# Moving the V loads of a cached-attention decode kernel from SyncE's DMA queue to ScalarE's

## The chip, the cores and the metric

The kernel runs on one core of a Trainium2 chip. The metric is device time in microseconds (us), lower is better, as the median of several executions. On one core a run counts as slow when it is over 1.5% above the fastest of the same kernel. In the profiles PE is TensorE, DVE VectorE, ACT ScalarE and SP SyncE; PEld is TensorE's weight load, and SPq and ACTq are the DMA issues of SyncE and ScalarE.

## The reference, cut to what matters

One decode step: four sequences, one new token each, attention over a window of cached keys and values, plus a gated feed-forward block on the same normalized input.

```python
B, Sq, D = 4, 1, 640
Hq, Hkv, Sk, Dh = 32, 32, 8192, 192        # window W = 2048 of 8192 positions
xn = layernorm(x)
q = (xn @ wq) per head
scores = einsum("bhqd,bhkd->bhqk", q, k[last W]) * Dh ** -0.5
o = einsum("bhqk,bhkd->bhqd", softmax(scores), v[last W])
return x + o.reshape(B, 1, Hq * Dh) @ wo + (silu(xn @ w1) * (xn @ w3)) @ w2
```

K and V are bf16. Per head, the four sequences' windows are 3.15 MB of K and 3.15 MB of V. Over 32 heads that is 201 MB, read once; with the weights 223 MB. There is little arithmetic per byte, so the DMA is the first suspect.

## The kernel before

Head by head, K and V arrive as one tile each of 128 partitions x 24,576 bytes. VectorE multiplies K by the broadcast q in four quarters; TensorE and VectorE reduce the products to scores; ScalarE takes the exponential; TensorE multiplies by V ("PV", into `o_ps`); ScalarE copies the result to `o_raw`.

```python
KBUFS = 2; VBUFS = 3; L = 10; GQ = 4      # a head is GQ = 4 slots
kpool = tile_pool(name="kt", bufs=KBUFS)
vpool = tile_pool(name="vt", bufs=VBUFS)

def load_k(h):
    kt = kpool.tile([P, NJ, Dh], BF16, tag="kt")
    nc.sync.dma_start(out=kt..., in_=k_win[:, h]...)
def load_v(h, pieces=1):
    vt = vpool.tile([P, NJ, Dh], BF16, tag="vt")
    ...
        nc.sync.dma_start(out=vt..., in_=src...)
# wo_load, ffn_load, w2_load, and the loads of x and Wq: nc.sync.dma_start too
...
for h in range(H):
    u0, ul = h * GQ, h * GQ + GQ - 1
    if h >= KBUFS:
        add((h - KBUFS + 1) * GQ, 0, load_k, h)       # K(h): after the last multiply of head h-2
    add(h * GQ + (2 if h != H - 3 else 5), 0, load_v, h, 1 if h < H - 1 else 2)
    ...                                              # multiply, add, reduce, softmax
    add(u0 + L, 3, pv, h, 0)                          # PV ten slots after the head began
    add(u0 + L + 2, 3, pv, h, 1)                      # its end frees V's buffer
for hg in range(NG):                                  # 8 groups of 4 heads
    add(hg * HG * GQ + 8 if hg < NG - 1 else NU, 0, wo_load, hg)
    ...
add(f, 0, ffn_load, "w1", B_w1)                       # f: head 6
add(f + 6, 8, ffn_load, "w3", B_w3)
add(NU + 2, 1, w2_load, [(0, FC // 2), (FC // 2, FC - 2), (FC - 2, FC)])
```

`add(slot, phase, ...)` fixes each engine's program order; semaphores fix the time. So a K issue waits for VectorE to free one of two buffers, and a V issue for a PV that frees one of three.

## Time and profile before

| | before |
|---|---|
| median of 4 runs | 533.83 us (532.94 to 534.59) |
| span of the profiled run | 533.2 us |
| VectorE busy / PE busy / ScalarE busy | 349 / 391 / 48 us |
| last byte loaded (from the packet records; the recorded texts have 524.6 and 524.7) | 525.5 us |

The page's table of DMA queues (bytes moved, and packet time as a share of 16 engines' span):

```profile
q1 hardware_dynamic: 11680, 222.97, 97.8%
```

The table of stretches of the kernel before: stretch, its length, busy time of PE, PEld, DVE, ACT and GpSimd (with their instructions), the clock granted to TensorE, DMA share, GB/s.

```profile
40.00:110.00 70.00, 50.16 (x331) 21.27 (x329) 50.65 (x64) 4.83 (x16) 0.00 (x0) 0.80 1.01 432
110.00:180.00 70.00, 51.68 (x379) 22.45 (x378) 43.06 (x58) 11.52 (x25) 0.00 (x0) 0.85 1.00 431
390.00:460.00 70.00, 50.07 (x378) 22.08 (x377) 44.62 (x61) 5.01 (x20) 0.00 (x0) 0.80 1.00 430
460.00:500.00 40.00, 32.73 (x237) 14.16 (x237) 30.71 (x40) 1.96 (x8) 0.00 (x0) 0.75 0.96 410
```

The DMA engines never rest from 40 to 460 us; the kernel is bound by bytes over rate. A line of the waits list of the kernel before (who waited for whom, us in total, times, longest):

```profile
DVE pr L202 <- DMA kt<-in_A_k_cache_dram: 99.2, 29, 7.9
```

And the last line of the view of the V tile of the same kernel:

```profile
DMA to landing us min/median/max: 12.5/25.6/30.3
```

VectorE waits for K 29 times in 32 heads. A V tile needs 25.6 us from issue to landing although its bytes take 7.3 us at 430 GB/s. The rest it stands in the queue, behind other tiles.

### The profile page before, as it was taken

The page shows a single profiled execution, that of the slowest core. Times are in us where ns is not written, and L with a number is a line of the kernel's source. Part 1 is how long each engine was busy: PE and PEld are TensorE (multiplying, and loading weights), DVE is VectorE, ACT ScalarE, POOL GpSimd, SP SyncE. Part 2 cuts the span into 40 slices and gives each one's busy share as a digit, 9 for nine tenths or more (in the row PEclk, how much of TensorE's full clock was granted, in tenths as well). Part 3 has the DMA queues.
Part 4 walks back from the last instruction along what each step waited for, and adds up shares of the span by engine and source line. Part 5 has one row for each costly group of instructions (what it writes and reads, how often), then busy time and mean ns, then how long its engine had stood idle before and what let it go on. Part 6 is the DMA issues. An engine that isn't in the chain of part 4 may idle for free.

```text
span 533.2 us, 6724 instructions
## 1 busy us (share of the span) xinstructions
PE 391.0 (73%) x2949; PEld 177.6 (33%) x2949; DVE 349.4 (66%) x471; ACT 48.2 (9%) x150; POOL 1.1 (0%) x8
## 2 busy tenths in 40 slices
PE   2876776867686978676947688586749868587987
PEld 0322232333142433232413334233313324232544
DVE  3177775787384776776757777578657778477860
ACT  2111000000222000000000000000000000000010
POOL 0000000000000000000000000000000000000000
PEclk9879776899698797688989969689996769777998
DMA  8999999999999999999999999999999999998993
GB/s 353 430 428 431 421 442 424 438 435 428 425 435 432 428 433 431 431 427 439 429 428 431 435 426 438 430 428 435 430 433 428 433 428 440 435 420 372 422 390 140
DMA packets 11709, 223.39 MB, mean 419 GB/s; under 512 B 1304, under 2 KB 1312, under 8 KB 2720
## 3 DMA queue, kind: packets, MB, share of 16 engines
q1 hardware_dynamic: 11680, 222.97, 97.8%
q8 instruction: 23, 0.38, 0.3%
q14 instruction: 6, 0.05, 0.0%
HBM read 222.96 MB, written 0.01 MB: 418 GB/s over the span
## 4 chain that ended last, share of the span: by engine, by line
DMA 59%; DVE 22%; PE 17%; issue 1%; ACT 0%; SPq 0%
DMA kt<-in_A_k_cache_dram 56%; DVE pr L202 17%; PE ps L213 7%; PE gp L294 5%; DVE sc L221 4%; DMA wt<-in_A_wq_dram 3%; PE qps L172 2%; PE o_ps L266 1%; PE acc_239 L194 1%; PE acc_240 L195 1%; DVE oT L303 1%; DVE rtb L284 1%; DVE qbc L178 0%; ACT o_raw L272 0%; DVE o_ps L186 0%
## 5 line engine op out<-in xcount | busy, mean ns | idle before, releaser
L213 PE MATMUL ps<-pr,idb 128*128 128x512 bf16 x768 | 228.9, 445 | 119.8 <-DVE sc L221 116.3
L202 DVE TENSOR_TENSOR pr<-kt,qbc 128x3072 bf16<-128x3072 bf16 x128 | 223.9, 1750 | 100.2 <-DMA kt<-in_A_k_cache_dram 99.2
L213 PEld LDWEIGHTS <-idb 128*128 128x128 bf16 x768 | 79.5, 108 | 219.8 <-issue 166.7
L221 DVE TENSOR_REDUCE sc<-ps 128x16 f32<-128x512 f32 x128 | 87.5, 684 | 10.1 <-PE ps L213 9.1
L266 PE MATMUL o_ps<-vt,z 128*8 128x384 bf16 x1024 | 59.3, 356 | 0.0
L294 PEld LDWEIGHTS gp<-sel,o_raw 128*32 128x32 f32 x768 | 46.8, 151 | 21.3 <-issue 19.2
L272 ACT COPY o_raw<-o_ps 128x384 f32<-128x384 f32 x32 | 15.3, 479 | 405.4 <-PE o_ps L266 405.4
L294 PE MATMUL gp<-sel,o_raw 128*32 128x4 f32 x768 | 49.6, 199 | 1.1 <-ACT o_raw L272 0.6
L266 PEld LDWEIGHTS <-z 128*8 128x8 bf16 x1024 | 21.1, 89 | 41.6 <-issue 32.6
L284 DVE RECIPROCAL rtb<-mt 32x4 f32<-32x4 f32 x32 | 5.7, 179 | 32.2 <-PE gp L294 31.9
L172 PE MATMUL qps<-wt,xnT 128*128 128x512 bf16 x60 | 17.7, 463 | 4.9 <-DMA wt<-in_A_wq_dram 4.9
L178 DVE CAST qbc<-qps 128x512 bf16<-128x512 f32 x6 | 3.8, 684 | 19.4 <-PE qps L172 19.4
L257 DVE TENSOR_TENSOR z<-ex,mask_b 128x256 bf16<-128x256 bf16 x32 | 13.2, 414 | 2.4 <-ACT ex L249 2.4
L194 PE MATMUL acc_239<-wo_t,oT 128*4 128x320 bf16 x48 | 13.8, 305 | 0.3 <-DVE oT L303 0.3
L195 PE MATMUL acc_240<-wo_t,oT 128*4 128x320 bf16 x48 | 13.8, 306 | 0.0
L243 PEld LDWEIGHTS mt<-ones_ff,gneg 1*128 1x128 f32 x64 | 9.4, 182 | 10.2 <-issue 9.6
L243 PE MATMUL mt<-ones_ff,gneg 1*128 1x1 f32 x64 | 12.1, 256 | 0.0
L172 PEld LDWEIGHTS <-xnT 128*128 128x128 bf16 x60 | 6.9, 115 | 15.3 <-issue 10.2
L249 ACT ACTIVATE ex<-sc,negm 128x64 bf16<-128x64 f32 x32 | 11.1, 348 | 1.0
L326 PE MATMUL gt<-w_756,xnT 128*4 128x512 bf16 x15 | 6.9, 622 | 4.2 <-DVE oT L303 2.9
L230 PE MATMUL mt<-idf,lmax 128*1 128x128 f32 x32 | 9.2, 287 | 0.0
L235 DVE TENSOR_REDUCE gmax<-mt 1x4 f32<-1x128 f32 x32 | 8.6, 269 | 0.7 <-PE mt L230 0.7
(59 smaller groups left out, 98.4 us busy)
## 6 DMA issues: line engine op xcount, KB each, us to landing
kt<-in_A_k_cache_dram SPq DMA_DIRECT2D x32, 3072.0 KB, 20.5
vt<-in_A_v_cache_dram SPq DMA_DIRECT2D x31, 3072.0 KB, 25.7
wo_t<-in_A_wo_dram SPq DMA_DIRECT2D x8, 960.0 KB, 19.4
wt<-in_A_wq_dram SPq DMA_DIRECT2D x2, 3072.0 KB, 9.8
vt<-in_A_v_cache_dram SPq DMA_DIRECT2D x2, 1536.0 KB, 14.1
w_756<-in_B_w_dram SPq DMA_DIRECT2D x1, 1920.0 KB, 23.4
w_1001<-in_B_w_dram SPq DMA_DIRECT2D x1, 1920.0 KB
wt<-in_A_wq_dram SPq DMA_DIRECT2D x1, 1536.0 KB, 19.8
```

The source lines that it names most:

```text
L172: nc.tensor.matmul(qp[:], lhsT=xnT[:, kc].rearrange("p a b -> p (a b)"), rhs=wq_rows[kc][:, (c0 + i) * QC:(c0 + i + 1) * QC], start=(kc == ...
L194: nc.tensor.matmul(acc0[:], lhsT=lhsT, rhs=rhs[:, 0:N0], start=first, stop=last)
L195: nc.tensor.matmul(acc1[:], lhsT=lhsT, rhs=rhs[:, N0:D], start=first, stop=last)
L202: nc.vector.tensor_tensor(out=pr[:], in0=kts[h][:, g * JQ:(g + 1) * JQ, :], in1=qbc[:, h * Dh:(h + 1) * Dh].unsqueeze(1).to_broadcast([P, ...
L213: nc.tensor.matmul(ps[:], lhsT=idb[:], rhs=pr[:, :, kk * DD:(kk + 1) * DD], start=(kk == 0), stop=(kk == NK - 1))
L221: nc.vector.tensor_reduce(out=scs[h][:, g * JQ:(g + 1) * JQ], in_=pss.pop(u)[:], axis=AX.X, op=ALU.add)
L243: nc.tensor.matmul(mt[:, P:P + 1], lhsT=gneg[:].rearrange("o p b -> o (p b)"), rhs=ones_ff[0:1, 0:1], start=True, stop=True)
L249: nc.scalar.activation(out=ex[:], in_=scs.pop(h)[:], func=ACTF.Exp, bias=negm[:, 0:1], scale=SCALE, accum_out=rsum[:])
L257: nc.vector.tensor_tensor(out=z[:], in0=ex[:].unsqueeze(2).to_broadcast([P, NJ, B]), in1=mask_b[:].unsqueeze(1).to_broadcast([P, NJ, B]), ...
L266: nc.tensor.matmul(o_ps[c * CT:c * CT + 2 * B, :], lhsT=z[:, 2 * jj:2 * jj + 2, :], rhs=vt[:, 2 * jj:2 * jj + 2, :], start=(jj < 4), stop= ...
L272: nc.scalar.copy(out=o_raw[:].rearrange("q two d -> q (two d)"), in_=o_ps[:])
L294: nc.tensor.matmul(gp[sl, i, :], lhsT=o_raw[:, part, i:Dh:RPP], rhs=sel[:, part * B:(part + 1) * B], start=(part == 0), stop=(part == 1))
```

## The change

The intent: V gets a queue of its own, so that V and K need not stand behind each other and SyncE's waits for K buffers do not hold up V.

```diff
-            nc.sync.dma_start(out=vt[:, i * n:(i + 1) * n, :].rearrange("q j d -> q (j d)"),
+            nc.scalar.dma_start(out=vt[:, i * n:(i + 1) * n, :].rearrange("q j d -> q (j d)"),
                               in_=src[:, :, i * n:(i + 1) * n, :].rearrange("p b j d -> p b (j d)"))
```

## The prediction

> **What bounds the kernel now.** The DMA engines. The queue table has SyncE's queue busy for 97.8% of the span, 418 GB/s in the mean; a table of stretches shows 430 to 432 GB/s from 13 to 460 us. The chain of waits is 56% "DMA kt", and the waits list has VectorE idle 99 us for K. VectorE needs 10.9 us of work per head (349 us / 32); K and V of a head (6.29 MB) need 14.6 us at 430 GB/s. Bytes stop at about 524.6 us; the last 8.6 us are a PE chain (last PV, o_raw, gp, oT, Wo and W2 products).
>
> **What the change does.** No byte and no compute instruction goes. 33 V issues (0.54 us each, 18 us) move from SyncE to ScalarE, which is 9% busy. SyncE's waits before V issues go, but cost nothing now: K lands 20.5 us and V 25.7 us after issue, so the queue is never empty. On ScalarE a V issue meets no new wait: its buffer is freed by PV matmuls whose o_raw copy ScalarE has already waited for. It comes 1.2 to 2.7 us later (o_raw 0.48, negm 0.17, exp 0.35, its accumulator 0.19, sometimes a table load 1.28).
>
> Order changes. One FIFO of K, V, K, V becomes two queues. The Trainium skill, "DMA: Bandwidth & Descriptors", section "Issuing engines are not separate DMA queues", says both run on the same 16 engines and interleave: no bandwidth gained; section "Queues, rings and completion order" has each engine alternate between queues by packet. This trace has one data queue and cannot confirm it. A K tile then flows at half rate, for 14.6 us instead of 7.3, but continuously: VectorE still gets one K per 14.6 us. The steady state stays equal.
>
> **Where I expect a loss.**
> 1. Weights sit on K's queue, so K falls behind V around W1, W3 and Wo; V fills its buffers and stops issuing. The backlog at a K issue, now about 11 us (3.6 of the K before, 7.3 of V), shrinks to an estimated 3 to 5 us, so pauses around the FFN (VectorE idle 8.6 us behind PE near 146 us) may leave bubbles: 0 to 3 us.
> 2. The end. Now the order is K31, V29, V30, V31, Wo, W2. Afterwards SyncE issues Wo and W2 right behind K31 (about 486 us instead of 504), competing with V30 and V31. K31 lands an estimated 2 us later than needed (503 against 500.7 us), V31 at an estimated 522 to 525 us, where the last PV now starts at 519.7. As 9 to 10 us of PE work follow, that adds 2 to 5 us.
>
> The start gains nothing: V0 goes out after ScalarE's qbc copies (31 us instead of 26.8), still before the queue is empty (about 34 us).
>
> **Predicted time:** 538 us, range 532 to 546. Faster by over 2%: 0.02; within 2%: 0.87; slower by over 2%: 0.11.
>
> **What would show it.** Two data queues, V's 101 MB on the second; about 430 GB/s from 13 to 460 us; V issued on ScalarE; VectorE idle behind K 100 to 110 us; Wo 7 and W2 issued near 486 us; the last PV 2 to 5 us later, after a wait for V, with V among the last bytes.
>
> **What would make it wrong.** Two interleaved streams moving at another rate than one (2% of rate is about 10 us); a share between the queues far from equal; ScalarE blocked at a V issue so that exp and o_raw come late; mid-run bubbles over 3 us.

## The result, and the profile after

The changed kernel takes 558.70 us (median of 4 runs, 554.50 to 559.21) against 533.83: a ratio of 1.0449, 95% interval 1.0396 to 1.0503. Ratios here are the mean time of one kernel's fast runs over that of the other's of the same rounds, so not quite the ratio of the medians. It is slower by 4.5%, outside the predicted range. The result stays correct.

The queue table of the kernel after:

```profile
q1 hardware_dynamic: 6928, 122.30, 52.5%
q10 hardware_dynamic: 4752, 100.67, 42.1%
```

The same bytes on two queues, and the shares now add up to 94.6% of a longer span. The table of stretches:

```profile
40.00:110.00 70.00, 46.80 (x306) 20.09 (x305) 47.26 (x61) 4.83 (x16) 0.00 (x0) 0.76 1.00 422
110.00:180.00 70.00, 47.01 (x348) 20.12 (x346) 38.71 (x51) 11.53 (x25) 0.00 (x0) 0.88 0.95 399
390.00:460.00 70.00, 48.52 (x388) 22.37 (x386) 44.68 (x61) 5.10 (x20) 0.00 (x0) 0.83 0.97 411
460.00:500.00 40.00, 24.89 (x225) 12.26 (x225) 27.59 (x37) 1.96 (x8) 0.00 (x0) 0.91 0.97 407
500.00:510.00 10.00, 8.10 (x68) 4.21 (x68) 9.55 (x14) 0.98 (x4) 0.00 (x0) 1.00 0.65 242
```

Every stretch moves less than before. A finer view tells a lower rate from pauses: the same window of 80 us in 40 slices of 2 us, before and after (first row busy tenths of the DMA engines, second row GB/s).

```profile
DMA  9999999999999999999999999999999999999999
GB/s 406 418 442 467 430 406 414 442 467 418 406 418 455 467 418 406 418 467 415 403 480 426 422 406 418 504 418 414 393 430 504 406 418 406 430 504 406 418 406 438
```

```profile
DMA  9999999999999268999999999999999999999999
GB/s 462 467 426 406 393 455 479 430 406 393 455 479 430 123 172 356 451 406 467 406 430 442 418 467 406 430 438 406 416 405 508 441 393 442 418 467 438 393 446 406
```

These are 400 to 480 us. Outside a hole of 5 us at 426 us (123, 172, 356 GB/s) the two move at the same pace. So the streams do not disturb each other; the engines now and then have nothing to do. Summing over all packet records how far the rate of each half microsecond fell short of its median, where it was under 80% of it (median 432 GB/s in both kernels; the first 5 us left out):

```
         lost in gaps   where (us from the start: us lost)
before      2.7 us      483-487: 1.9   510-513: 0.7
after      19.1 us      103-109: 1.2   148-155: 5.1   240-244: 1.3   303-305: 0.7   364-367: 0.7
                        426-431: 2.6   490-494: 1.7   499-506: 4.9   and two of 0.3 to 0.4 at the end
```

The last byte loaded comes at 543.0 us instead of 525.5 (17.5 us later, of which the gaps are 16.4), and the work behind it lasts 14.4 us instead of 7.7. Together 24.2 us: the whole difference of the spans. Two places to explain, then: the gaps and the end.

**The gaps.** The same line of the waits list of the kernel after:

```profile
DVE pr L202 <- DMA kt<-in_A_k_cache_dram: 117.7, 28, 11.2
```

And of its view of the V tile:

```profile
DMA to landing us min/median/max: 13.2/19.0/25.6
```

V lands sooner (19.0 instead of 25.6 us), as intended, and nobody is served by it: the time from V's landing to its first PV grew from 15.4 to 21.1 us (medians of heads 3 to 28, from issue, landing and matmul times in the trace). A landed tile occupies its buffer without being work for the DMA engines. Bytes issued but not yet moved, over all queues:

```
                                          before   after
median just before a K issue (MB)            4.1     2.6
K issues (of 29) that find under 1 MB          1       7
mean from 40 to 480 us (MB)                  7.1     5.1
```

The seven K issues that find under 1 MB are at 102, 240, 302, 364, 428, 490 and 503 us: one at each gap except that at 148 us. That one is the feed-forward's. Three lines of the timeline of the kernel after (start, length, engine, line; in brackets the idle time before):

```profile
143.59 2.29 PE L326 MATMUL gt<-w_756,xnT 128*4 128x512 bf16 x5 [3.42 <-DMA w_756<-in_B_w_dram]
...
151.83 0.54 ACTq L100 DMA_DIRECT2D vt<-in_A_v_cache_dram  x1
152.25 0.55 SPq L91 DMA_DIRECT2D kt<-in_A_k_cache_dram  x1
```

W1 shares the DMA with V and lands 28.2 us after issue (23.4 before). PE waits 3.4 us for it, then runs the W1 products, and until 151.8 us neither a V nor a K buffer comes free while both queues run dry.

The packet records also show what a weight does at the head of K's queue. From 515 to 530 us rows of Wo and W2 (7,680 bytes each) moved on it beside rows of V (24,576 bytes each): 191 rows against 195, so 98 GB/s against 331. In mid-run it is the same: from 330 to 334 us, around a Wo, 49 rows moved on each queue. While such a weight moves, V's queue draws three quarters of the bandwidth, and a K behind the weight waits. The gaps fit this: but for the one at 148 us, each of those from 103 to 490 us with over 0.5 us lost begins 32 to 34 us after a Wo began to move. How much of the gaps this share explains, no run tested.

**The end.** DMA issues on SyncE ("SPq") and ScalarE ("ACTq") in the timeline, before and after:

```profile
484.90 0.54 SPq L91 DMA_DIRECT2D kt<-in_A_k_cache_dram  x1
485.54 18.31 SPq L100 DMA_DIRECT2D vt<-in_A_v_cache_dram  x4
503.90 0.58 SPq L106 DMA_DIRECT2D wo_t<-in_A_wo_dram  x1
504.52 1.42 SPq L350 DMA_DIRECT2D w_3883<-in_B_w_dram  x3
```

```profile
490.13 13.01 SPq L91 DMA_DIRECT2D kt<-in_A_k_cache_dram  x2
503.64 0.35 SPq L106 DMA_DIRECT2D wo_t<-in_A_wo_dram  x1
504.04 1.49 SPq L350 DMA_DIRECT2D w_3883<-in_B_w_dram  x3
506.19 0.54 ACTq L100 DMA_DIRECT2D vt<-in_A_v_cache_dram  x1
506.78 0.63 ACTq L100 DMA_DIRECT2D vt<-in_A_v_cache_dram  x1
517.88 0.54 ACTq L100 DMA_DIRECT2D vt<-in_A_v_cache_dram  x1
518.46 0.62 ACTq L100 DMA_DIRECT2D vt<-in_A_v_cache_dram  x1
```

Before, V29, V30 and V31 (two pieces; the merged line of four) stand ahead of the last Wo and W2. After, Wo and W2 go out right behind K31 and take bandwidth from V29 to V31. What waits last, in the chain of waits of the kernel after:

```profile
518.46 24.63 DMA vt<-in_A_v_cache_dram
543.13 1.48 PE o_ps L266 x16
544.63 0.49 ACT o_raw L272
```

V31's second piece lands at 543.1 us, nearly together with W2's last, and all of head 31's last work comes after it.

### The profile page after: what moved, and what is told of

Its sections match the earlier page's. It is cut to its first block, busy times and chain, and to the rows that moved or that the text cites. A ratio compares the mean times of both kernels' runs of the same rounds, so it can differ in the third digit from the quotient of the medians.

```text
span 557.4 us, 6720 instructions
## 1 busy us (share of the span) xinstructions
PE 381.9 (69%) x2948; PEld 175.8 (32%) x2949; DVE 349.4 (63%) x471; ACT 48.3 (9%) x150; POOL 1.1 (0%) x8
## 4 chain that ended last, share of the span: by engine, by line
DMA 62%; DVE 21%; PE 14%; issue 1%; ACT 0%; SPq 0%; ACTq 0%
DMA kt<-in_A_k_cache_dram 50%; DVE pr L202 15%; DMA w_756<-in_B_w_dram 5%; PE ps L213 5%; DMA vt<-in_A_v_cache_dram 4%; PE gp L294 4%; DVE sc L221 4%; DMA wt<-in_A_wq_dram 3%; PE qps L172 2%; PE gt L326 1%; PE acc_239 L194 1%; PE acc_240 L195 1%; DVE rtb L284 0%; PE o_ps L266 0%; DVE oT L303 0%
## 5 line engine op out<-in xcount | busy, mean ns | idle before, releaser
L213 PE MATMUL ps<-pr,idb 128*128 128x512 bf16 x768 | 216.7, 427 | 146.7 <-DVE sc L221 143.4
L213 PEld LDWEIGHTS <-idb 128*128 128x128 bf16 x768 | 77.6, 105 | 241.6 <-issue 184.1
L272 ACT COPY o_raw<-o_ps 128x384 f32<-128x384 f32 x32 | 15.3, 479 | 429.2 <-PE o_ps L266 429.2
L194 PE MATMUL acc_239<-wo_t,oT 128*4 128x320 bf16 x48 | 14.6, 319 | 0.3 <-DVE oT L303 0.3
L195 PE MATMUL acc_240<-wo_t,oT 128*4 128x320 bf16 x48 | 14.6, 320 | 0.0
L172 PEld LDWEIGHTS <-xnT 128*128 128x128 bf16 x60 | 6.8, 114 | 15.4 <-issue 10.3
L303 DVE TENSOR_TENSOR oT<-gp,rtb 32x24 bf16<-32x24 f32 x32 | 5.6, 176 | 9.3 <-PE gp L294 8.6
## 6 DMA issues: line engine op xcount, KB each, us to landing
w_756<-in_B_w_dram SPq DMA_DIRECT2D x1, 1920.0 KB, 28.2
```

The source lines that it names most:

```text
L172: nc.tensor.matmul(qp[:], lhsT=xnT[:, kc].rearrange("p a b -> p (a b)"), rhs=wq_rows[kc][:, (c0 + i) * QC:(c0 + i + 1) * QC], start=(kc == ...
L194: nc.tensor.matmul(acc0[:], lhsT=lhsT, rhs=rhs[:, 0:N0], start=first, stop=last)
L195: nc.tensor.matmul(acc1[:], lhsT=lhsT, rhs=rhs[:, N0:D], start=first, stop=last)
L213: nc.tensor.matmul(ps[:], lhsT=idb[:], rhs=pr[:, :, kk * DD:(kk + 1) * DD], start=(kk == 0), stop=(kk == NK - 1))
L272: nc.scalar.copy(out=o_raw[:].rearrange("q two d -> q (two d)"), in_=o_ps[:])
```

## The experiments

Theory A: the loss comes from sharing. Two queues are served side by side, so the less urgent tile (V) lands early, sits in its buffer, and stops being a reserve of queued bytes; the weights on K's queue hurt K further. Rival B: the loss comes from ScalarE, which issues V late because o_raw, negm and exp come first in its program. Rival C, that two streams from HBM are slower than one, already falls with the finer view above: outside the gaps the rate is the same.

Every kernel gave a correct result. "In flight" below is the median of bytes issued and not yet moved just before a K issue; the kernel before was run beside each group (532.83, 534.45 and 533.44 us), and the ratios are to it. The changed kernel was not run again: differences from its 558.70 us compare runs of different groups, and its own four runs spread over 4.7 us.

### The two engines exchanged

```diff
-        nc.sync.dma_start(out=kt[:]...          # and Wq, Wo, W1, W3, W2
+        nc.scalar.dma_start(out=kt[:]...
         ... V stays on nc.sync, as in the kernel before
```

> Two queues with the roles exchanged: K, Wq, Wo, W1, W3, W2 go out on ScalarE, V on SyncE, which has nothing else to do. Theory A (two queues share the DMA engines about equally, so V lands early, sits in its buffers, and the bytes queued ahead at a K issue shrink): the same loss as the change, 552 to 562 us, gaps in the DMA traffic again near W1 and before each Wo. Rival B (V goes out late because ScalarE must first do o_raw, negm and exp): back near 534 to 540 us, since V now goes out the moment its buffer is free and K's issue waits on VectorE in either place.

560.18 us (555.23 to 561.57), ratio 1.049 (1.0438 to 1.0542). In flight 2.4 MB, 23.6 us lost in gaps. V now never waits for ScalarE's work, and the loss is all there. B is not needed for it, and does not explain it.

### Everything on ScalarE's queue

```diff
 after:
-        nc.sync.dma_start(out=kt[:]...          # and Wq, Wo, W1, W3, W2
+        nc.scalar.dma_start(out=kt[:]...
         ... V on nc.scalar, as in the change
```

> One queue again, but ScalarE's: K, V and the weights all go out on ScalarE, V at the same place in its program as in the change. Theory A: one FIFO keeps a V tile behind each K, so the time returns to 533 to 539 us and the median outstanding at a K issue to about 4.4 MB. Rival B (issuing on ScalarE is what costs): no better than the change, 555 us or more, since now K also waits in ScalarE's order.

533.34 us (532.92 to 534.05), ratio 1.0005 (0.9984 to 1.0025). V goes out at the same place of ScalarE's program as in the change, K too, and nothing is lost. Its queue table:

```profile
q10 hardware_dynamic: 11664, 222.96, 98.0%
```

In flight 4.6 MB, 1.8 us in gaps. With the two runs above, the four placings of K and V on two engines are complete: both on one engine 533.8 or 533.3 us, one on each 558.7 or 560.2 us. What counts is the number of queues, not which engine issues.

### The weights behind V

```diff
 after:
-        nc.sync.dma_start(out=wo_t[:]...        # and W1, W3, W2
+        nc.scalar.dma_start(out=wo_t[:]...
```

> The change, with Wo, W1, W3 and W2 moved to ScalarE's queue behind V; K is alone on SyncE. Theory A with its second part (the weights delay K on its own queue while V is served beside them, which drains V and sets off the gap some heads later): the gaps near 148 us and before each Wo shrink, and at the end Wo 7 and W2 come after V31 again: 538 to 546 us. If the weights' place does not matter and the equal share alone is to blame: 554 us or more.

539.28 us (537.51 to 543.03), ratio 1.0116 (1.0059 to 1.0174): most of the loss goes. The gap at 148 us and those of 240 to 430 us are gone; 8.5 us of gaps are left (1.7 at 181 us), 5.6 of them at 486 to 494 us, where V29's late slot leaves only K30 queued. So it matters which tiles share a queue: K with nothing in front of it is hurt less, and here it is the weights, on V's queue, that draw the small share beside K. The order of the end is restored in this run as well, so it mixes two effects; they are parted below.

### V29 at the regular slot

```diff
 after:
-        add(h * GQ + (2 if h != H - 3 else 5), 0, load_v, ...
+        add(h * GQ + 2, 0, load_v, ...
```

> The change, with V29 issued at the regular slot instead of three slots later. Theory A: the gap of about 5 us between 499 and 506 us, in which only K30 was queued, goes, because V29 is in the queue from about 490 us: 551 to 555 us, 4 to 6 us less than the change. If the gap at the end came from K alone (VectorE behind), no difference.

556.01 us (553.71 to 559.45), ratio 1.0434, a miss: 2.7 us less than the change by the medians and under 1 us by the ratios (1.0434 against 1.0449), which is not clear of the spread. The gap at 499 to 506 us went, and the last byte came at 536.4 instead of 543.0 us. But with V29 and V30 competing, K31 landed only at 520.6 us (515.9 in the change), and VectorE stood still for it:

```profile
520.62 1.76 DVE L202 TENSOR_TENSOR pr<-kt,qbc 128x3072 bf16<-128x3072 bf16 x1 [6.21 <-DMA kt<-in_A_k_cache_dram]
```

A filled gap was paid for by a wait elsewhere: the bytes came sooner, the urgent ones later.

### Both of these

```diff
 after:
-        nc.sync.dma_start(out=wo_t[:]...        # and W1, W3, W2
+        nc.scalar.dma_start(out=wo_t[:]...
-        add(h * GQ + (2 if h != H - 3 else 5), 0, load_v, ...
+        add(h * GQ + 2, 0, load_v, ...
```

> The change with both repairs: all weights but Wq behind V on ScalarE's queue, and V29 at the regular slot. The weights alone left 539.3 us with one gap of 5.6 us at 486 to 494 us, in which V29 had not been issued. Theory A: that gap goes, and as no weight competes with K31, 533 to 537 us. If the gap only turns into a wait for K31, as it did when V29 alone was moved: 538 us or more.

543.66 us (537.98 to 544.54), ratio 1.0151 (1.0091 to 1.0211, so unclear whether slower by 2%); a miss. The gap at 486 us is gone (3.3 MB in flight), but new ones stand at 504 to 527 us. Here ScalarE's program order does cost something:

```profile
518.63 0.48 ACT L272 COPY o_raw<-o_ps 128x384 f32<-128x384 f32 x1 [11.38 <-PE o_ps L266]
...
519.22 0.33 ACTq L350 DMA_DIRECT2D w<-in_B_w_dram  x1
```

W2's issue stands behind an o_raw copy that waits 11.4 us for PE, so W2 goes out at 519.2 us (504.5 in the kernel before). That is rival B's mechanism, real for a load placed behind a wait, but not for V. The profiled run was the fastest of the four; why the other three took 543 to 545 us is open.

### More bytes in flight: K in halves

```diff
 after:
-    kpool = tile_pool(name="kt", bufs=KBUFS)
+    kpool = tile_pool(name="kt", bufs=KBUFS * 2)       # tiles of half the size: the same SBUF bytes
-            add((h - KBUFS + 1) * GQ, 0, load_k, h)
+            for i in range(2):                          # half 0 goes out two multiplies earlier
+                add((h - KBUFS) * GQ + (i + 1) * GQ // 2, 0, load_k, h, i)
     # load_k(h, i) loads one half; multiply g reads half g // 2
```

> The change, everything on its queue as in the change, but each K tile is two halves with buffers of their own (the same SBUF bytes): half 0 is issued again two multiplies before half 1. It puts on average about 0.8 MB more in flight at any time. Theory A (too few bytes outstanding): the gaps shrink, 542 to 551 us. If a lack of bytes in flight is not the cause (the order of service alone is): within 3 us of the change, 555 us or more.

542.80 us (542.37 to 544.33), ratio 1.0163 (1.0129 to 1.0197). No tile changed its queue, and 16 us came back. Over 420 us its DMA is busy again:

```profile
40.00:460.00 420.00, 300.01 (x2314) 135.84 (x2313) 286.25 (x376) 34.50 (x113) 0.00 (x0) 0.87 1.01 430
```

In flight 5.6 MB, 2.4 us lost in gaps, the last byte at 526.7 us. What is left is the end: 14.5 us follow that byte.

### The same halves on one queue

```diff
 before:
-    kpool = tile_pool(name="kt", bufs=KBUFS)
+    kpool = tile_pool(name="kt", bufs=KBUFS * 2)       # and the rest as in the experiment above
```

> The kernel before with the same halves of K. Its queue never ran low before 483 us, so theory A has nothing to mend in mid-run: 531 to 534 us, at best the 2 us of the one gap at 483 to 487 us. If halves are faster for another reason (the first multiply of a head starts when half the tile is there): 529 us or less.

532.95 us (531.88 to 534.17), ratio 0.9974 (0.9938 to 1.0010): the same. In flight rises to 8.6 MB and buys nothing, because the engines were never short. So halves are not faster by themselves where the queue is full; in the changed kernel they mend a shortage. They do two things at once: half of K is issued earlier, and VectorE can start on a half. Both free buffers sooner, and no run parts them.

### Both repairs and halves

```diff
 after, weights on nc.scalar, V29 at the regular slot:
-    kpool = tile_pool(name="kt", bufs=KBUFS)
+    kpool = tile_pool(name="kt", bufs=KBUFS * 2)       # and the rest as above
```

> Both repairs and the halves of K on two queues. Theory A: no gap is left in mid-run, so the time is bytes over rate as in the kernel before, plus the end: 530 to 535 us. Below 529 us would mean that two queues, once fed, beat one queue.

540.09 us (538.29 to 542.40), ratio 1.0121; a miss. Gaps were down to 3.1 us. The second half of K31 landed at 511.7 us (the whole tile at 495.9 us in the kernel before), and W2 again went out at 519.6 us behind ScalarE's waits. By the trace the end, not mid-run, held it; no run tested that.

### The order of the end alone

```diff
 after:
-    wo_load: nc.sync for every group;           slot of the last: NU
+    wo_load: nc.scalar for the last group;      slot of the last: NU - 2, right behind V31
-    w2_load: nc.sync,   add(NU + 2, 1, ...)
+    w2_load: nc.scalar, add(NU - 2, 1, ...)
```

> The change, with the order of the end alone restored: Wo 7 and W2 leave SyncE's queue and go out on ScalarE's right behind V31. The gaps of mid-run stay. If the loss is the sum of two parts (gaps of about 16 us, and an end about 6 us longer because W2 competes with V30 and V31 and V31 comes last), this gives back only the second: 551 to 555 us. If the end costs nothing by itself: 557 us or more.

552.49 us (551.82 to 553.24), ratio 1.035 (1.0326 to 1.0374): 6.2 us back. The gaps stayed (19.3 us), the last byte too (544.0 us), but it is W2's now: the last PV starts at 537.4 instead of 543.1 us, and 7.4 us follow the last byte instead of 14.4.

### Halves and the order of the end

```diff
 after, with the edit above:
-    kpool = tile_pool(name="kt", bufs=KBUFS)
+    kpool = tile_pool(name="kt", bufs=KBUFS * 2)       # and the rest of the halves
```

> The change with both parts mended and nothing else: K in halves (which left the last DMA byte at 526.7 us, against 524.7 in the kernel before, but the end at 542.8) and the order of the end restored. If the two parts are the whole loss: 534 to 538 us, at most 1% over the kernel before. If something else of the second queue is left: 539 us or more.

536.27 us (534.13 to 538.43), ratio 1.005 (1.0022 to 1.0079). The two repairs alone gave 15.9 us (558.70 - 542.80) and 6.2 us (558.70 - 552.49), in sum 22.1; together they give 22.4 (by the ratios 15.3, 5.3 and 21.3 us). So they add up, to nearly the whole loss of 24.9 us. V is still on ScalarE's queue and every other load but the last four on SyncE's. The 0.5% that remains shows as 5.9 us of gaps, 3.1 of them at 492 to 497 us, where V29's late slot leaves only K queued, and 1.0 at 152 us.

### A try at better than both

```diff
 before, with K in halves:
-        add(h * GQ + (2 if h != H - 3 else 5), 0, load_v, ...
+        add(h * GQ + 2, 0, load_v, ...
```

> The kernel before (one queue) with K in halves and V29 at the regular slot, a try at a version better than both. The bytes bound it: the last byte at about 524 us and some 8 us of matrix work after it. 530 to 534 us, so at most 0.5% under the kernel before; 535 us or more if V29 then pushes K31 back.

533.63 us (532.76 to 535.22), ratio 1.0003 (0.9983 to 1.0022): no gain. The gap of the kernel before at 483 to 487 us is gone (halves alone had closed it), and the last byte stays at 525.6 us. No version beat the kernel before.

## Why the prediction was wrong

- *The DMA engines bound the kernel.* Right: 430 to 432 GB/s and a share of 1.00 before.
- *No bandwidth gained, and the two queues interleave.* Right, and shown here: the rate outside the gaps stayed at 432 GB/s, and in 261 separate microseconds of the changed kernel in which both queues held over 0.4 MB and moved rows of K and V alone, K drew 221 and V 210 GB/s. But the half rate that the prediction gives to K's queue does not hold beside a weight: there it was 98 of 429 GB/s.
- *On ScalarE a V issue meets no new wait.* Right for V: the exchange of engines and the all-on-ScalarE kernel show that the issuing engine costs nothing.
- *The steady state stays equal.* Wrong. Seven K issues in 29 found under 1 MB and the engines paused. VectorE idled 118 us for K, not the 100 to 110 foretold.
- *Mid-run bubbles: 0 to 3 us.* This is the step that failed: 11.6 us were lost in gaps before 460 us, where the kernel before lost none. The mechanism stood in the prediction (weights on K's queue, V ahead, a shrunken backlog), and the backlog was even underrated: foretold 3 to 5 us of work, measured 2.6 MB, or 6.0 us at 432 GB/s. What was mis-sized was what a thin reserve costs. A median reserve of 6 us does not cover the dips, which come at W1 and 32 to 34 us after the start of the other Wo. With the gaps of 490 to 506 us and the last small ones, all gaps cost 16.4 us more than before. That the thin reserve is the cause is shown by halves: 16 us back without moving a tile between queues, and nothing gained where the reserve was ample.
- *V29 in the queue with K31.* The prediction had Wo and W2 compete with V30 and V31 and named no gap there. Between V28 (472.6 us) and V29 (506.2 us) no V was issued. The slot had been chosen for one queue, where the gap at that place is 1.9 us; here it left K30 alone, and 4.9 us were lost from 499 to 506 us, until K31 and V29 moved.
- *The end: 2 to 5 us.* Right in mechanism (Wo and W2 go out behind K31 and compete; V among the last bytes), a little small: 6.2 us by experiment (5.3 by the ratios).
- *The start gains nothing.* Nothing contradicts it: 344 GB/s in the first 13 us (348 before), 431 to 40 us (430).

The split of the gaps between Wo and W1/W3 was not tested one by one, and the experiment that moved the weights moved the end too. That V landing early is what thins the reserve is read from the trace (15.4 to 21.1 us from landing to use); no run forced V to land late on its own queue.

## What to carry to other kernels

When the DMA engines are saturated, a single FIFO in the order of need is a schedule: the less urgent load waits in the queue, where it is also the reserve that keeps the engines busy. Splitting it over two queues let that load land early here and idle in its buffer, so count the bytes still to be moved at each issue (here 4.1 against 2.6 MB), look at the dips and not the mean, and check every order that was tuned for one queue, above all the end. If a second queue is needed, free the buffers of the urgent tiles in smaller pieces and restore the order of the last loads: these two took the loss from 4.5% to 0.5%. Keeping the weights off the urgent queue and restoring the end in one step took it to 1.2%; all of it together, with V29 at its regular slot, was no better than 1.2% either.

## What the Trainium skill lacked or had wrong

- "DMA: Bandwidth & Descriptors", section "Issuing engines are not separate DMA queues", says that several issuing engines only save the sequencer's issue time. The runs agree that no bandwidth is won (432 GB/s either way), but the page does not say that it can cost: 558.70 against 533.83 us for the same bytes, by the gaps and the end shown above.
- The same page, section "Queues, rings and completion order", has each engine take its queues in turn by packet, with several descriptors to a packet. The runs agree with turns: 221 and 210 GB/s with rows of 24,576 bytes on both. What the section does not say is that the queue with the shorter rows then gets fewer bytes. With rows of 7,680 bytes against V's of 24,576 from 515 to 530 us, nearly equal numbers of rows moved (191 and 195), so the queue of the weights drew 98 and V's 331 GB/s: 23%, where turns of equally many rows would give 24%. How many rows make a turn, no run here shows.
- The same page, section "Where 436 GB/s comes from", says that for transfers between HBM and SBUF the HBM side, about 358 GB/s, binds. That sentence leaves out what the page says elsewhere, that the limit is for both cores of a pair loading at once. This one core loaded at 430 to 432 GB/s for 400 us; no run here loads with two. "HBM Reference", section "Specifications (TRN2)", has it right: a core streaming alone measures well above its share.
- No page that I read tells how much must stand in the queue to keep the engines busy. In the changed kernel a pause came at each K issue that found under 1 MB, and one more at W1. The kernels without pauses in mid-run had medians of 4.1 MB and more, or, with the weights off K's queue and V29 at its regular slot, 3.3 MB; but a median is no guarantee: halves with the order of the end restored had 5.5 MB and still one pause of 1.0 us at 152 us.
